# A linear-attention and MLP kernel: new load order and head-half work in the first batch, other slots for batch 3, a 384+128 last chunk

## The chip, the cores and the metric

The kernel runs on one core of a Trainium2 chip. The metric is the device time of one execution in microseconds; of several runs the median is taken. Times in a profile count from the first instruction of the profiled execution; its span ends with the last instruction, and the execution's own time is a little longer.

## The reference

For 8 batches of 8 heads, 576 tokens and a head size of 64, linear attention is computed, and its output goes through a two-layer MLP with the tanh form of gelu:

```
phi(x) = where(x > 0, x, exp(x) - 1) + 1
kv  = phi(k)^T v          # per head, 64 x 64
z   = sum over tokens of phi(k)
num = phi(q) kv ;  den = phi(q) . z + 1e-6
x   = num / den           # heads side by side: 4608 tokens x 512
out = gelu_tanh(x @ w_in) @ w_out     # w_in 512 x 2048, w_out 2048 x 512
```

Inputs and output are float32; the kernel multiplies in bfloat16.

## The kernel before, in words

**Tiling.** Each batch has 512 main tokens (4 chunks of 128) and a rest of 64. The main tokens of batch b make block j = b of the MLP; the rests of all eight batches together make a ninth block of 512 tokens, block 8. The attention of a block is: exponentials on ScalarE (ACT), phi on VectorE (DVE, `phi_into`, L176: `max(x,0) + min(exp(x),1)`), a cast of v beside a column of ones (`cast_v` L204, `cast_vr` L212 for the rest), five matmuls for each of four head pairs into `kv_ps` (`kv_mm`, L220 and L227), two copies of the diagonal 64-row blocks into the block-diagonal `kvbd` (`kv_evac`, L243; `second` names another engine for the second block), transposes of phi(q) to `qt`, four matmuls for each chunk into `n_ps` (`nab_mm`, L254), a reciprocal and a product on DVE (`nab_evac`, L264 and L266), and a transpose of x to `xt`. The rests have the same steps, two batches in one tile (`plan_rest`, with the transposed `qtr` and the output `xt_rest`).

**The MLP.** `first_half(j)` makes 16 row blocks m of h: four matmuls of 512 columns each (L302), then gelu on ACT (L685). `second_half(j)` runs 16 groups of four matmuls into `o_ps` (L728), copies the result and stores it. For the last quarter of block 8 `last_chunk` makes the output in column pieces (L697, copy L706, stores L709).

**The order of the work.** It is written out by hand: each engine runs its instructions in program order, and so do the queues of SyncE (SP), which issues most loads and the transposing DMAs, and of GpSimd (POOL), which issues later loads of the rests and casts the weights (L150, L157). `at(phase, j, slot, fn)` puts attention work of later batches behind slot `slot` of `first_half(j)` (phase 1) or `second_half(j)` (phase 2); within one slot it runs in the order in which the plan functions were called. `plan_second`, `plan_third` and `plan_attention(3, ...)` place batches 1, 2 and 3; batch 3's kv and nab work stands in `first_half(2)`.

**Buffers.** Loads of k, q, v and weight stages share six buffers (`pld`, tag `ld`). PSUM has four one-bank buffers `ps_ho` and two two-bank buffers `ps_a`; in block 0, h for m = 0 to 3 goes to `ps_ho` and m = 4 to 7 to `ps_a`.

**The start.** SP issues the loads of batch 0, the first rests, batch 1's k and the first two column blocks of w_in (L113 to L123). Meanwhile `keep_warm` (L329) runs matmuls on zeros. Then exponentials, phi, transposes of q through TensorE (`transpose_q`, L337, with a copy at L338), the v cast, kv, the evacuation, nab and the transposes of x follow. `first_mm_early` makes h for the first half of the tokens. The exponentials of batch 1's k (L401, L405) stand on ACT before the gelu table is loaded (L146), and that before the first gelu. In `plan_second`, `last_w_out` casts half of the last block of w_out on ACT (L157) behind batch 1's `kv_evac`.

Of the kernel before, what the change touches and what calls it, by code (L numbers as in the profile page):

```python
# [15 lines left out]
def kernel(  # L16
# [12 lines left out]
    nc = tc.nc  # L29
# [33 lines left out]
    def load_main(src, b, name, eng, parts=1):  # L63
        t = pld.tile([P, H, C * D], FP32, name=name, tag="ld")
        hs = H // parts
        for i in range(parts):
            eng.dma_start(  # L67
                out=t[:, i * hs : (i + 1) * hs, :],
                in_=src[b, i * hs : (i + 1) * hs, 0:MAIN, :].rearrange(
                    "h (p c) d -> p h (c d)", c=C  # L70
                ),
            )
        return t

    def load_rest_half(src, t, m, s, eng):
        eng.dma_start(  # L76
            out=t[REST * s : REST * (s + 1)],
            in_=src[2 * m + s, :, MAIN:S, :].rearrange("h p d -> p h d"),
        )
# [4 lines left out]
            load_rest_half(src, t, m, s, eng)  # L84
        return t

    def load_w_in(i, parts=1):
        t = pld.tile([P, KM, 512], FP32, name="w_st", tag="ld")
        n = 512 // parts
        for u in range(parts):  # L90
            nc.sync.dma_start(  # L91
                out=t[:, :, n * u : n * (u + 1)],
                in_=w_in_r[:, :, 512 * i + n * u : 512 * i + n * (u + 1)],
            )
        return t

    def load_w_out(i):
# [18 lines left out]
    for n in ("kr", "vr", "qr"):  # L116
        ld[n, 0] = prest.tile([P, H, D], FP32, name=n[0] + "_r")
    load_rest_half(k, ld["kr", 0], 0, 0, nc.sync)
    ld["v", 0] = load_main(v, 0, "v_x", nc.sync, parts=2)
    load_rest_half(v, ld["vr", 0], 0, 0, nc.sync)  # L120
    ld["k", 1] = load_main(k, 1, "k_x", nc.sync)
    load_rest_half(k, ld["kr", 0], 0, 1, nc.sync)
    w_st = [load_w_in(0, 2), load_w_in(1)]  # L123


    ident = const.tile([P, P], BF16, name="ident")
# [210 lines left out]
            nc.tensor.transpose(t_ps[:, c, 0, :], src(c, i), ident)  # L337
        copy(out=qt[:, :, i, :], in_=t_ps[:, :, 0, :])  # L338

    for n, e, s in (  # L340
        ("k", ke, halves[0]),
        ("k", ke, halves[1]),
        ("q", qe, halves[0]),
        ("kr", kre, None),
        ("q", qe, halves[1]),
    ):
        if s is None:
            exp_rest_half(n, e, 0)
        else:
            nc.scalar.activation(e[:, s], ld[n, 0][:, s], AF.Exp)  # L350
    keep_warm(36)
    phi_into(kp, ld["k", 0], ke, halves[0])
    phi_into(kp, ld["k", 0], ke, halves[1])
    phi_into(qp, ld["q", 0], qe, halves[0])
    phi_rest_half("kr", kre, 0)
    cast_v(0, nc.scalar.copy, halves[0])
    for i in range(2):
        transpose_q(i, nc.scalar.copy)
    keep_warm(5)
    phi_into(qp, ld["q", 0], qe, halves[1])  # L360
    cast_v(0, nc.scalar.copy, halves[1])
    cast_vr(0, (0,))
    for i in range(2, NP):
        transpose_q(i, nc.vector.tensor_copy)
    keep_warm(2)
    for i in range(NP):
        if i % 2 == 0:
            kv_ps = ps_a.tile([P, 2, 512], FP32, name="kv_ps", tag="a")
        kv_mm(0, i, kv_ps, i % 2)
        if i % 2 == 1:  # L370
            kv_evac(0, kv_ps[:, 0:1], i // 2, nc.scalar.copy)
    keep_warm(1)
    for i in range(2):
        cast_w_in_halves(i)
# [22 lines left out]
    nab0(1)  # L397
    keep_warm(2)
    tx0(0)
    ke1 = pe.tile([P, H, C * D], BF16, name="k_e")  # L400
    nc.scalar.activation(ke1[:, 0:2], ld["k", 1][:, 0:2], AF.Exp)  # L401
    nab0(2)
    keep_warm(1)
    tx0(1)
    nc.scalar.activation(ke1[:, 2:H], ld["k", 1][:, 2:H], AF.Exp)  # L405
    kre1 = pe.tile([P, H, D], BF16, name="kr_e")
    exp_rest_half("kr", kre1, 1)
    gelu_table()
# [29 lines left out]
    def at(ph, j, slot, fn):  # L438
        fill.setdefault((ph, j, slot), []).append(fn)
# [66 lines left out]
            at(ph, j, s_n[c], lambda c=c: nab(c))  # L506
            at(ph, j, s_n[c], lambda c=c: tx(c))

    def plan_rest(m, j0, j1, s1):
        box = {}  # L510

        def tq():
            box["qt"] = psm.tile([P, NP, P], BF16, name="qtr")
            nc.sync.dma_start_transpose(
                out=box["qt"],
                in_=phi["qr", m][:, 0].rearrange("p h d -> p (h d)"),
            )

        def nab():
            n_ps = ps_a.tile([P, 2, 512], FP32, name="n_ps", tag="a")  # L520
            for h in range(2):
                nab_mm(box["qt"], kvbds[(2 * m + h) % 4], n_ps, slice(REST * h, REST * (h + 1)))
            x = nab_evac(n_ps)
            nc.sync.dma_start_transpose(
                out=xt_rest[:, :, P * m : P * (m + 1)],
                in_=x.rearrange("p a t d -> p (a t d)"),
            )

        at(*j0, tq)
        at(1, j1, s1, nab)  # L530

    def plan_second():

        b = 1
        box = {}

        def exps():
            box["q"] = pe.tile([P, H, C * D], BF16, name="q_e")
            for s in halves:
                nc.scalar.activation(box["q"][:, s], ld["q", b][:, s], AF.Exp)  # L540
            gelu_table()

        def phis():
            phi["q", b] = pphi.tile([P, C, H, D], BF16, name="q_p")
            for s in halves:
                phi_into(phi["q", b], ld["q", b], box["q"], s)

        def cast_vs():
            cast_vr(0, (1,))
            cast_v(b, nc.vector.tensor_copy)  # L550

        def last_w_out():
            cast_w_out_halves(3, (nc.gpsimd.tensor_copy, nc.scalar.copy))
            load_rests(1, (("kr", k), ("vr", v)))
            for s in range(2):
                load_rest_half(q, ld["qr", 0], 0, s, nc.gpsimd)
            load_rests(1, (("qr", q),))

        def kv():
            kv_ps = ps_a.tile([P, 2, 512], FP32, name="kv_ps", tag="a")  # L560
            for i in range(NP):
                kv_mm(b, i, kv_ps)
            kv_evac(b, kv_ps, second=nc.scalar.copy)

        def tq(h):
            if h == 0:
                box["qt"] = pt.tile([P, C, NP, P], BF16, name="qt")
            t_ps = ps_a.tile([P, 4, NP, P], BF16, name="t_ps", tag="a")
            t_q(q_src(b), None, 2 * h, 2, t_ps)
            copy = nc.vector.tensor_copy if h else nc.scalar.copy  # L570
            copy(out=box["qt"][:, 2 * h : 2 * h + 2], in_=t_ps[:, 0:2])

        def nab(c):
            n_ps = ps_a.tile([P, 2, 512], FP32, name="n_ps", tag="a")
            nab_mm(box["qt"][:, c], kvbds[b], n_ps)
            box["x", c] = nab_evac(n_ps)

        def tx(c):
            copy = nc.scalar.copy if c < 2 else nc.vector.tensor_copy
            pe_tx(b, c, box["x", c], c < 2, copy)  # L580

        def early(m):
            first_mm_early(1, m)

        at(1, 0, 11, exps)
        at(2, 0, 0, phis)
        at(2, 0, 0, cast_vs)
        for fn, c, slot in (
            (tq, 0, 7), (tq, 1, 7), (lambda c: kv(), 0, 10), (lambda c: last_w_out(), 0, 10),
            (nab, 0, 11), (nab, 1, 12), (nab, 2, 13), (tx, 0, 13), (nab, 3, 14),  # L590
            (tx, 1, 14), (tx, 2, 15), (early, 0, 15), (early, 1, 15), (tx, 3, 15),
            (early, 2, 15),
        ):
            at(2, 0, slot, lambda fn=fn, c=c: fn(c))
# [94 lines left out]

    def last_chunk(g, u):  # L690

        if u % 2 == 1:
            return
        o_ps = ps_ho.tile([P, d_model], FP32, name="o_ps", tag="ho")
        t, f = C - 1, slice(128 * u, 128 * u + 256)
        for m in range(MM):
            nc.tensor.matmul(  # L697
                o_ps[:, f],
                lhsT=g[:, m, P * t : P * (t + 1)],
                rhs=w_out_sb[:, m, f],  # L700
                start=(m == 0),
                stop=(m == MM - 1),
                skip_group_check=True,
            )
        o_sb = pld.tile([P, 1, 512], FP32, name="o_last", tag="ld")
        nc.vector.tensor_copy(o_sb[:, 0, f], o_ps[:, f])  # L706
        for s, eng in ((0, nc.sync), (1, nc.scalar)):
            r0 = (2 * t + s) * S + MAIN
            eng.dma_start(  # L709
                out=out[r0 : r0 + REST, f], in_=o_sb[REST * s : REST * (s + 1), 0, f]  # L710
            )
# [39 lines left out]
    plan_prepare(  # L751
        3, (2, 1, 7), (2, 1, 15), None, (1, 2, 0), (1, 2, 1), None, (2, 1, 12)
    )
    plan_attention(3, 1, 2, (4, 5, 6, 7), (11, 12, 13, 14))
    for b in range(4, B):
        j = b - 2
        plan_prepare(
            b, (1, j, 15), (2, j, 1), (2, j, 2), (2, j, 3), (2, j, 5), (2, j, 8), (2, j, 8)
        )
        plan_attention(b, 1, b - 1, (1, 2, 3, 4), (6, 8, 10, 12))  # L760
    plan_rest(0, (1, 2, 3), 2, 15)
    at(2, 1, 7, lambda: box0.__setitem__("qr", phi_rest("qr", 1)))
    at(1, 2, 8, lambda: box0["qr"]())
    plan_rest(1, (2, 2, 8), 3, 14)
    for b in range(4, B):
        at(2, b - 3, 2 if b == 4 else 0, lambda b=b: load_batch(b))
    for m in range(2, 4):
        at(2, 2 * m - 3, 3, lambda m=m: load_rests(m, (("kr", k), ("vr", v))))
        at(1, 2 * m - 2, 9, lambda m=m: load_rests(m, (("qr", q),)))
    for m in range(2, 4):  # L770
        plan_rest(m, (2, 2 * m - 2, 9), 2 * m, 14)

    for j in range(B + 1):
        first_half(j)
# [29 lines left out]
```

## Time and profile before

| what | value |
| --- | --- |
| median of 5 runs | 300.46 us (298.78 to 302.07) |
| the profiled execution | 298.78 us, its span 297.0 us |
| granted TensorE clock | 0.999 |
| first h matmul of block 0 | 20.64 us |
| first o_ps matmul of block 0 | 35.01 us |
| first half of block 2, with batch 3's attention | 85.73 to 103.72 us |
| last matmul | 293.03 us |
| DVE, ACT, POOL busy | 132.3, 159.2, 37.9 us |

In the profile PE is TensorE's matmuls and PEld its weight loads, DVE is VectorE, POOL is GpSimd, SP is SyncE, and a q behind an engine means its sequencer, which issues DMAs. A line of the timeline has start, length, engine, source line, operation, out<-in, shape and count; in brackets is the idle time before it and what ended it. Matmul lengths include the pipeline, so the array's time is read from start to start.

### The profile page before, as it was taken

The numbers are of one execution on the slowest core, as the hardware profiler recorded it, in microseconds if no ns is written. First come the engines' busy times: TensorE is split into PE (matmuls) and PEld (weight loads), VectorE is DVE, ScalarE is ACT, GpSimd is POOL, SyncE is SP. The second block draws the span as 40 slices with busy tenths as digits, with TensorE's granted clock in tenths as the row PEclk, the third lists the DMA queues.
The fourth block names the chain that finished last, engine by engine and source line by source line (L and its number), as shares of the span: only waits on it lengthen the run. The fifth ranks groups of instructions, "written<-read, shape, count | busy, mean of one in ns | idle before, by whom it ended". The sixth has DMA issues, their size and how long they took to land.

```text
span 297.0 us, 4320 instructions
## 1 busy us (share of the span) xinstructions
PE 287.8 (97%) x1698; PEld 149.8 (50%) x1698; DVE 132.3 (45%) x244; ACT 159.2 (54%) x222; POOL 37.9 (13%) x56
## 2 busy tenths in 40 slices
PE   8889999999999899999999999999999999999995
PEld 6775455644564444554455445544544444444444
DVE  2979494228689478244714493438142000000002
ACT  4658934679964572567356825682561067017500
POOL 8028658300002400000000000000000000000000
PEclk9999999999999999999999999999999999999999
DMA  7999999991498999736933696203341110021033
GB/s 250 339 379 406 392 370 372 320 373 58 112 347 248 172 237 352 163 68 202 349 108 55 194 356 142 53 20 106 106 54 36 71 71 2 0 83 58 2 71 72
DMA packets 64260, 53.24 MB, mean 179 GB/s; under 512 B 31728, under 2 KB 57584, under 8 KB 64240
## 3 DMA queue, kind: packets, MB, share of 16 engines
q1 hardware_dynamic: 60816, 41.82, 49.0%
q10 hardware_dynamic: 2464, 8.52, 7.4%
q0 software_dynamic: 960, 2.62, 3.8%
q8 instruction: 13, 0.21, 0.3%
q14 instruction: 7, 0.06, 0.1%
HBM read 36.70 MB, written 9.44 MB: 155 GB/s over the span
## 4 chain that ended last, share of the span: by engine, by line
PE 86%; DMA 5%; SPq 4%; DVE 2%; issue 1%; POOL 1%; ACT 0%; ACTq 0%
PE o_ps L728 40%; PE h_ps L302 38%; DMA w_st<-in_moe_w_in_dram 3%; PE n_ps L254 2%; SPq L67 2%; PE kv_ps L220 2%; DMA qtr<-qr_p 2%; SPq L76 2%; PE o_ps L697 1%; DVE k_p L176 1%; SPq L91 1%; PE t_ps L277 1%; PE kv_ps L227 1%; POOL w_in_sb L150 1%; DVE kvbd L243 0%
## 5 line engine op out<-in xcount | busy, mean ns | idle before, releaser
L728 PE MATMUL o_ps<-w_out_sb,g 128*128 128x512 bf16 x560 | 124.6, 379 | 0.2 <-ACT w_out_sb L157 0.2
L302 PE MATMUL h_ps<-xt,w_in_sb 128*128 128x512 bf16 (+1 forms) x548 | 119.8, 365 | 0.3
L685 ACT ACTIVATE g<-h_ps 128x512 bf16<-128x512 f32 x144 | 83.8, 598 | 50.9 <-PE h_ps L302 48.2
L728 PEld LDWEIGHTS <-g 128*128 128x128 bf16 x560 | 54.1, 98 | 63.3 <-issue 0.5
L302 PEld LDWEIGHTS <-w_in_sb 128*128 128x128 bf16 x612 | 57.6, 98 | 54.9 <-issue 0.5
L743 ACT COPY o_sb<-o_ps 128x512 f32<-128x512 f32 x18 | 10.5, 585 | 55.5 <-PE o_ps L728 55.5
L741 DVE COPY o_sb<-o_ps 128x512 f32<-128x512 f32 x17 | 11.7, 688 | 62.4 <-PE o_ps L728 62.3
L266 DVE TENSOR_TENSOR x<-n_ps,r 128x512 bf16<-128x512 f32 x36 | 24.9, 691 | 1.2
L176 DVE SCALAR_TENSOR_TENSOR k_p<-k_x,k_e 128x512 bf16<-128x512 f32 (+1 forms) x36 | 22.9, 697 | 0.3
L176 DVE SCALAR_TENSOR_TENSOR q_p<-q_x,q_e 128x512 bf16<-128x512 f32 (+1 forms) x40 | 22.4, 622 | 0.3
L264 DVE RECIPROCAL r<-n_ps 128x8 f32<-128x8 f32 x36 | 7.4, 206 | 27.4 <-PE n_ps L254 27.4
L243 DVE CAST kvbd<-kv_ps 64x260 bf16<-64x260 f32 (+1 forms) x15 | 6.1, 409 | 28.0 <-PE kv_ps L227 28.0
L172 DVE TENSOR_SCALAR k_e<-k_e 128x2048 bf16<-128x2048 bf16 (+1 forms) x9 | 5.7, 635 | 22.3 <-ACT k_e L167 17.7
L329 PE MATMUL w_ps<-warm 128*128 128x252 bf16 x94 | 13.7, 310 | 1.1 <-DVE warm L128 1.1
L254 PEld LDWEIGHTS <-qt 128*128 128x128 bf16 x128 | 9.7, 98 | 8.7 <-issue 1.4
L302 PE MATMUL h_ps<-xt_rest,w_in_sb 128*128 128x512 bf16 x64 | 14.0, 379 | 0.0
L254 PE MATMUL n_ps<-kvbd,qt 128*128 128x130 bf16 x128 | 12.7, 221 | 1.2 <-DMA qt<-q_p 0.7
L220 PEld LDWEIGHTS <-k_p 128*128 128x128 bf16 x128 | 9.7, 96 | 6.3 <-issue 0.9
L220 PE MATMUL kv_ps<-vp,k_p 128*128 128x130 bf16 x128 | 11.8, 220 | 0.6 <-DVE vp L204 0.6
L204 DVE CAST vp<-v_x 128x2048 bf16<-128x2048 f32 x7 | 8.6, 1222 | 8.7 <-DMA v_x<-in_v_dram 8.7
L150 POOL CAST w_in_sb<-w_st 128x1024 bf16<-128x1024 f32 x8 | 10.4, 1329 | 13.9 <-DMA w_st<-in_moe_w_in_dram 13.9
L146 ACT ACT_TABLE_LOAD x8 | 10.3, 1283 | 3.3 <-DVE o_sb L741 2.8
(61 smaller groups left out, 153.9 us busy)
## 6 DMA issues: line engine op xcount, KB each, us to landing
out_dram<-o_sb ACTq DMA_DIRECT2D x16, 512.0 KB, 3.5
k_x<-in_k_dram SPq DMA_DIRECT2D x7, 1024.0 KB, 6.0
v_x<-in_v_dram SPq DMA_DIRECT2D x7, 1024.0 KB, 11.7
q_x<-in_q_dram SPq DMA_DIRECT2D x6, 1024.0 KB, 9.3
w_st<-in_moe_w_out_dram SPq DMA_DIRECT2D x4, 1024.0 KB, 11.5
w_st<-in_moe_w_in_dram SPq DMA_DIRECT2D x3, 1024.0 KB, 9.3
q_x<-in_q_dram SPq DMA_DIRECT2D x4, 512.0 KB, 9.2
k_x<-in_k_dram SPq DMA_DIRECT2D x2, 512.0 KB, 4.2
```

Source lines behind the costliest of these rows:

```text
L146: nc.scalar.preload_act_table_set("gelu_apprx_tanh_and_others")
L150: nc.gpsimd.tensor_copy(out=w_in_sb[:, :, 512 * i + 256 * u : 512 * i + 256 * (u + 1)], in_=w_st[i][:, :, 256 * u : 256 * (u + 1)],)
L176: nc.vector.scalar_tensor_tensor(xp[:, c, hs, :], xv[:, c, hs, :], 0.0, ev[:, c, hs, :], op0=ALU.max, op1=ALU.add,)
L220: nc.tensor.matmul(dst, lhsT=kp[:, c, P * i : P * (i + 1)], rhs=vps[b % 2][:, 2 * i : 2 * i + 2, c, :], start=(c == 0), stop=False,)
L254: nc.tensor.matmul(n_ps[rows, i // 2, 2 * E * (i % 2) : 2 * E * (i % 2) + 2 * E], lhsT=qt_c[:, i, rows], rhs=kvbd[:, i, :], skip_group_che ...
L266: nc.vector.tensor_tensor(x, n_v[:, :, :, 0:D], r[:, :, :, None].to_broadcast([P, 2, 4, D]), op=ALU.mult,)
L302: nc.tensor.matmul(h_ps[:, tok], lhsT=w_in_sb[:, c, P * m : P * (m + 1)], rhs=xt[:, c, tok], start=(c == 0), stop=(c == KM - 1), skip_grou ...
L329: nc.tensor.matmul(w_ps[:, 0:252], lhsT=warm[:, 0:P], rhs=warm)
L685: nc.scalar.activation(gs[j][:, i, :], ps, AF.Gelu_apprx_tanh)
L728: nc.tensor.matmul(o_pss[t], lhsT=g[:, m, P * t : P * (t + 1)], rhs=w_out_sb[:, m, :], start=(m == 0), stop=(m == MM - 1),)
L741: nc.vector.tensor_copy(dst, o_ps)
L743: nc.scalar.copy(dst, o_ps)
```

## The change

It has five parts. In the first batch the rest of v is loaded ahead of v, v stays behind k and q, w_in's first block and half of its second go ahead of batch 1's k, and the other half behind it; the exponentials and phi of k's rest move behind those of q; all copies of `qt` are ACT's; and kv runs by halves of the heads, where the second half of v is cast by DVE (heads 4 and 5) and ACT (6 and 7) after the first half's evacuation. The exponential of batch 1's k is one instruction, behind both ACT copies of `xt`. `kv_evac` of batch 1 stays wholly on DVE. Batch 3's kv and nab each move one slot on, and the rest nab of batches 0 and 1 moves from slot 15 of `first_half(2)` to slot 2 of `second_half(2)`. The last chunk is made in columns 0 to 383 and 384 to 511.

```diff
-    def load_w_in(i, parts=1):
-        t = pld.tile([P, KM, 512], FP32, name="w_st", tag="ld")
-        n = 512 // parts
-        for u in range(parts):
-            nc.sync.dma_start(
-                out=t[:, :, n * u : n * (u + 1)],
-                in_=w_in_r[:, :, 512 * i + n * u : 512 * i + n * (u + 1)],
-            )
+    def load_w_in(i, t=None, f=slice(0, 512)):
+        if t is None:
+            t = pld.tile([P, KM, 512], FP32, name="w_st", tag="ld")
+        nc.sync.dma_start(
+            out=t[:, :, f], in_=w_in_r[:, :, 512 * i + f.start : 512 * i + f.stop]
+        )
         return t
...
     load_rest_half(k, ld["kr", 0], 0, 0, nc.sync)
+    load_rest_half(v, ld["vr", 0], 0, 0, nc.sync)
     ld["v", 0] = load_main(v, 0, "v_x", nc.sync, parts=2)
-    load_rest_half(v, ld["vr", 0], 0, 0, nc.sync)
+    w_st = [load_w_in(0), load_w_in(1, None, slice(0, 256))]
     ld["k", 1] = load_main(k, 1, "k_x", nc.sync)
     load_rest_half(k, ld["kr", 0], 0, 1, nc.sync)
-    w_st = [load_w_in(0, 2), load_w_in(1)]
+    load_w_in(1, w_st[1], slice(256, 512))
...
-    for n, e, s in (
-        ("k", ke, halves[0]),
-        ("k", ke, halves[1]),
-        ("q", qe, halves[0]),
-        ("kr", kre, None),
-        ("q", qe, halves[1]),
-    ):
-        if s is None:
-            exp_rest_half(n, e, 0)
-        else:
+    for n, e in (("k", ke), ("q", qe)):
+        for s in halves:
             nc.scalar.activation(e[:, s], ld[n, 0][:, s], AF.Exp)
+    exp_rest_half("kr", kre, 0)
     keep_warm(36)
-    phi_into(kp, ld["k", 0], ke, halves[0])
-    phi_into(kp, ld["k", 0], ke, halves[1])
-    phi_into(qp, ld["q", 0], qe, halves[0])
-    phi_rest_half("kr", kre, 0)
-    cast_v(0, nc.scalar.copy, halves[0])
+    for n, xp, e in (("k", kp, ke), ("q", qp, qe)):
+        for s in halves:
+            phi_into(xp, ld[n, 0], e, s)
     for i in range(2):
         transpose_q(i, nc.scalar.copy)
     keep_warm(5)
-    phi_into(qp, ld["q", 0], qe, halves[1])
-    cast_v(0, nc.scalar.copy, halves[1])
+    phi_rest_half("kr", kre, 0)
+    cast_v(0, nc.scalar.copy, halves[0])
     cast_vr(0, (0,))
     for i in range(2, NP):
-        transpose_q(i, nc.vector.tensor_copy)
+        transpose_q(i, nc.scalar.copy)
     keep_warm(2)
-    for i in range(NP):
-        if i % 2 == 0:
-            kv_ps = ps_a.tile([P, 2, 512], FP32, name="kv_ps", tag="a")
-        kv_mm(0, i, kv_ps, i % 2)
-        if i % 2 == 1:
-            kv_evac(0, kv_ps[:, 0:1], i // 2, nc.scalar.copy)
+    for h in range(2):
+        if h == 1:
+            cast_v(0, nc.vector.tensor_copy, slice(4, 6))
+            cast_v(0, nc.scalar.copy, slice(6, 8))
+        kv_ps = ps_a.tile([P, 2, 512], FP32, name="kv_ps", tag="a")
+        for i in range(2):
+            kv_mm(0, 2 * h + i, kv_ps, i)
+        kv_evac(0, kv_ps[:, 0:1], h, nc.scalar.copy)
...
     tx0(0)
-    ke1 = pe.tile([P, H, C * D], BF16, name="k_e")
-    nc.scalar.activation(ke1[:, 0:2], ld["k", 1][:, 0:2], AF.Exp)
     nab0(2)
     keep_warm(1)
     tx0(1)
-    nc.scalar.activation(ke1[:, 2:H], ld["k", 1][:, 2:H], AF.Exp)
+    ke1 = exp_main("k", 1)
...
-    def plan_rest(m, j0, j1, s1):
+    def plan_rest(m, j0, j1):
...
-        at(1, j1, s1, nab)
+        at(*j1, nab)
...
-            kv_evac(b, kv_ps, second=nc.scalar.copy)
+            kv_evac(b, kv_ps)
...
-        if u % 2 == 1:
+        if u > 1:
             return
...
-        t, f = C - 1, slice(128 * u, 128 * u + 256)
+        t, f = C - 1, (slice(0, 384), slice(384, 512))[u]
...
-    plan_attention(3, 1, 2, (4, 5, 6, 7), (11, 12, 13, 14))
+    plan_attention(3, 1, 2, (5, 6, 7, 8), (12, 13, 14, 15))
...
-    plan_rest(0, (1, 2, 3), 2, 15)
+    plan_rest(0, (1, 2, 3), (2, 2, 2))
...
-    plan_rest(1, (2, 2, 8), 3, 14)
+    plan_rest(1, (2, 2, 8), (1, 3, 14))
```

The call for m = 2 and 3 changes in the same way as that for m = 1, in form alone.

More of the change, by code (lines that the diff above doesn't have):

```diff
@@ L770 @@
     for m in range(2, 4):
-        plan_rest(m, (2, 2 * m - 2, 9), 2 * m, 14)
+        plan_rest(m, (2, 2 * m - 2, 9), (1, 2 * m, 14))
     for j in range(B + 1):
```

## The prediction

> **What bounds the kernel now.** I read the page first, then TensorE's waits, then its timeline around each wait, then the landings of the first DMAs (each issue's start plus its time to landing).
>
> The page:
>
> ```profile
> PE 287.8 (97%) x1698; PEld 149.8 (50%) x1698; DVE 132.3 (45%) x244; ACT 159.2 (54%) x222; POOL 37.9 (13%) x56
> L728 PE MATMUL o_ps<-w_out_sb,g 128*128 128x512 bf16 x560 | 124.6, 379 | 0.2 <-ACT w_out_sb L157 0.2
> ```
>
> TensorE is the bound: 97% of the span. Its matmuls overlap, so cost is start to start: 0.216 us for 512 columns (64 of them from 134.09 to 147.90), 0.109 for 256. Moving work on other engines gains nothing unless a TensorE gap closes. The waits, columns total, times, longest:
>
> ```profile
> PE n_ps L254 <- DMA qtr<-qr_p: 0.8, 1, 0.8
> PE n_ps L254 <- DMA qt<-q_p: 0.7, 1, 0.7
> PE kv_ps L220 <- DVE vp L204: 0.6, 1, 0.6
> PE o_ps L728 <- ACT w_out_sb L157: 0.2, 1, 0.2
> ```
>
> Four single waits, of which three fall into one stage, the first product of batch 2, where batch 3's attention is woven in. TensorE's timeline there (start, length, group):
>
> ```profile
> 87.68 1.67 PE L302 MATMUL h_ps<-xt,w_in_sb 128*128 128x512 bf16 x7
> 90.00 0.40 PE L220 MATMUL kv_ps<-vp,k_p 128*128 128x130 bf16 x4 [0.65 <-DVE vp L204]
> ...
> 99.64 1.02 PE L302 MATMUL h_ps<-xt,w_in_sb 128*128 128x512 bf16 x4
> 101.31 0.41 PE L254 MATMUL n_ps<-kvbd,qt 128*128 128x130 bf16 x4 [0.66 <-DMA qt<-q_p]
> 101.56 1.02 PE L302 MATMUL h_ps<-xt,w_in_sb 128*128 128x512 bf16 x4
> 103.36 0.44 PE L254 MATMUL n_ps<-kvbd,qtr 128*64 128x130 bf16 x8 [0.77 <-DMA qtr<-qr_p]
> 103.72 1.47 PE L728 MATMUL o_ps<-w_out_sb,g 128*128 128x512 bf16 x6
> ```
>
> Start to start the gaps are larger than the brackets. Seven matmuls from 87.68 are paid at 87.68+7x0.216=89.19, so kv lost 0.81; 99.64+4x0.216=100.50, so the nab for chunk 3 lost 0.82; 101.56+0.86=102.42, so the rest nab lost 0.93. Together 2.56 us.
>
> Two smaller gaps. At 48.77 o_ps waits 0.40 (47.94+2x0.216=48.37) for ACT's cast of w_out:
>
> ```profile
> 47.28 0.37 ACT L243 CAST kvbd<-kv_ps 64x260 bf16<-64x260 f32 x1 [3.70 <-DVE kvbd L243]
> 47.68 1.04 ACT L157 CAST w_out_sb<-w_st 128x1024 bf16<-128x1024 f32 x1
> ```
>
> The cast's data landed at 44.97, but ACT stood before it on kv_evac. And in the start, the chain that ended last goes
>
> ```profile
> 14.49 8.55 DMA w_st<-in_moe_w_in_dram
> 23.10 1.50 POOL w_in_sb L150
> 24.64 10.53 PE h_ps L302 x48
> ```
>
> 24 narrow matmuls from 21.74 are paid at 24.36, so w_in's second block costs 0.28. Before 20.64 the start is batch 0's attention chain, with TensorE fed by keep_warm.
>
> **What the skill says.** The Trainium skill, DMA: Bandwidth & Descriptors, "Queues, rings and completion order": on each DMA engine a ring's descriptors are taken in order. The trace agrees: SP's first sixteen transfers land in issue order (10.18, 10.96, 12.13, 13.80, 14.55, 17.45, 18.17, 19.18 ... for q, k_r, v, v, v_r, k, k_r, w_in), about 0.75 us per 128 KB rest and 2.55 per 1 MB. SBUF — State Buffer, "SBUF: two separate sides": a DVE instruction with two SBUF inputs and a GpSimd instruction exclude each other. Agrees: k_p takes 0.69 alone and 1.52 beside POOL's casts, which go from 1.04 to 1.49; PSUM-fed DVE work beside them stays at 0.69. TensorE: Matmul & The Clock Gate, "What's actually happening": the clock falls after about 3.4 us idle. The trace shows no such gap and a granted clock of 0.999.
>
> **The change, part by part.**
>
> *Batch 3 one slot on, rest nab three slots on.* kv moves from slots 4-7 to 5-8, nab from 11-14 to 12-15. TensorE reaches kv after one more h group, at 89.19+0.86=90.05; the vp cast ends at 89.95. Gap 0.81 goes, with 0.05 to spare. DVE's order (k_p, vp, q_p, qr_p, kv_evac, second qr_p) stays, and kv_evac is asked for 0.05 later, so qt's last transpose lands where it did, 101.27. Ten slots lie between kv and the last nab as before: TensorE arrives at 100.50+0.05=100.55 and still waits 0.77, until 101.31. But now h of slot 15 is behind it, and o_ps starts at 101.55. The rest nab comes after three o_ps groups, 101.55+3x0.86=104.14, past qtr's landing at 103.31: no wait. It keeps its 0.37 and its 0.09 of entry (the unstalled rest nabs of later batches show 0.09). Equivalent end 101.55+0.46=102.01 against 103.72: **-1.71**. Behind the rest nab: its evacuation (0.21+0.69) now stands on DVE after k_p and kr_p of batch 4 and before vp and q_p, and its transpose on SP after batch 5's loads and before qt. ACT's exponentials for batch 4 come about 1.9 earlier, so q_p comes 1.0 earlier nevertheless; qt landed at 121.98 for a nab at 124.91. xt_rest is used only at the end. Cost 0; 0.9 if that cover were gone.
>
> *kv_evac of batch 1 wholly on DVE.* A second DVE half takes 0.43 (batch 2: 0.42 and 0.43 back to back), ending at 46.76+0.87=47.63 against ACT's 47.65: nothing for nab. ACT, free since 43.58, casts w_out from 44.97 to 46.05; the need is 48.37. **-0.40**.
>
> *First batch.* Queue: v_r goes ahead of v, then w_in 0 and half of w_in 1, then k, k_r, the other half. Estimated landings, adding the steps above one after another from k_r's 10.96: v_r +0.75=11.7, v +1.3=13.0 and +1.6=14.6 (two halves took 2.84 with the step before), w_in 0 +2.6=17.2, half of w_in 1 +1.25=18.4, k +2.8=21.2, k_r +0.7=21.9, last half 23.05 as before, since as much lies ahead of it. ACT: exp of q's second half starts on landing, 10.2, not behind kr at 11.52; so DVE's q_p runs through from 9.53 and ends at 13.23 (14.49 before). kr_p to 14.15, vr cast to 14.49. ACT: two qt copies to 12.9, v heads 0-3 13.05-14.08 (1.03), two qt copies to 15.04. kv of the first pairs starts its last product at 14.83; evacuation, 0.32 later, on DVE 15.15-15.44, then ACT to 15.73. Only then v 4-5 on DVE (0.42, the 64x512 cast's row) to 15.82 and v 6-7 on ACT (0.58) to 16.28; kv of the last pair 16.33-16.56, evacuation 16.88-17.45. nab restarts at 17.50, not 17.26: +0.24. So halving the cast saves less than standing behind the first evacuation costs. DVE's three x follow 0.24 later; the third transposes end at 20.72. xt's second copy, no longer behind a piece of exp k (0.63 at 19.48), is ready at 20.67, so h starts at 20.72 against 20.64: +0.08. w_in's third cast (POOL, 1.04 each from 17.2) ends near 20.4, long before the 24.4 at which it is needed, and the 0.28 gap goes: **-0.20**. Both ends: -0.5 if v lands early enough for the DVE and ACT casts and the crossings between the engines are shorter than shown; +0.5 if v's first half lands 0.5 late, since ACT's cast of it then gates kv. TensorE idles 1.0 us once, far below 3.4. k late: exp k 21.2-23.1, kr to 23.7, table load 1.28 to 25.0, gelu 1.0 later than 23.94. Cover: h for m=0..7 has eight PSUM banks; m=8 starts at 27.9 and needs gelu 0 at 25.6. Later wo, q and v land as before, since the bytes ahead are the same. Phi k ends about 1 later, DVE idles 4.3 until 34.76.
>
> *Last chunk 384+128.* Matmuls 16x(0.163+0.058)=3.53 against 3.49 (0.163 between the measured widths, 0.058 from kv's 130 columns): +0.04. Last copy 0.29 (the 64x130 row) against 0.42; half the last store: up to -0.2. Together **-0.1**. The unshown 32 KB store: between no gain and 0.3.
>
> Sum -1.71-0.40-0.20-0.10=-2.4: span 297.0 to 294.6, this execution 298.78 to 296.4. It was the fastest of the five, 1.7 under the median; from the median 300.46 I get 298.0.
>
> **Rivals.**
>
> *B: a batch 3 wait only moves.* The margin at kv is 0.05, and transposes shown take 2.4 to 7.5 us to land, beside POOL's loads. If qt's last lands 0.9 later, the total is -1.5: 299.0. For: the wait for qt stays even in my sum, and the title says two slots where the diff moves one. Against: its issue follows an unchanged DVE order.
>
> *C: qt lands sooner.* If it lands 0.8 sooner, all 2.56 go, total -3.2: 297.3. A second slot would have given this; for it speaks only the scatter of landings.
>
> *D: slower, by the first batch.* v is last of the attention inputs and its second half gates kv. Once it lands after about 15.4 plus, each us is one us for TensorE; slower than before needs 15.4+2.4=17.8. It would have to lag its place in the queue by 3 us. Price at 18.8: +1.0, 301.5.
>
> **Chances.** Mine 0.57 (own range 297.2 to 298.9), B 0.20, C 0.18, D 0.05. Medians of this kernel scatter by some 0.7, so the range is 296.3 to 300.0. One per cent, about what a measurement can tell from no change, is 3.0 us: faster means under 297.46. That is two thirds of C and a third of mine: 0.30. Slower 0.03, within 0.67.
>
> **What would show it.** Right: no wait of kv on vp and of n_ps on qtr near 90-103, one of 0.6-0.7 on qt; w_out_sb cast by ACT ending near 46; h at 24.4 with no POOL wait; nab of batch 0 at about 17.5. Wrong: h waiting for ACT's gelu near 28, kv waiting for v past 16.5, a new wait in batch 4.

## The result and the profile after

Over the runs of one comparison the changed kernel takes 297.4 us (25 runs, 295.67 to 299.97) and the kernel before 299.41 us (46 runs, 297.1 to 302.97). The ratio is 0.994, with a 95% interval of 0.992 to 0.9959: faster by 1.8 us, between 1.2 and 2.4. The forecast was 298.0 from a median of 300.46, a ratio of 0.992, which lies at the edge of that interval. The ratios here and below, and the medians of the experiments, are over the runs in the fast state alone: beside the experiments 43 of 168 runs of the kernel before were in a slower one, of the kernel after none of 36, and no run here shows why. The profiled execution took 296.17 us with a span of 294.4, against 298.78 and 297.0. The two single profiles thus differ by 2.6 us, a little more than the ratio says.

TensorE is still the bound. The page's busy row and its costliest group:

```profile
PE 286.8 (97%) x1698; PEld 149.2 (51%) x1698; DVE 132.2 (45%) x244; ACT 159.7 (54%) x222; POOL 37.0 (13%) x56
L718 PE MATMUL o_ps<-w_out_sb,g 128*128 128x512 bf16 x560 | 124.6, 379 | 0.0
```

TensorE's work is the same to the instruction: 1698 matmuls, and the 560 of the output product sum to 124.6 again (L728 has become L718). Of that group only the idle time ahead of it went, from 0.2 to 0.0. So the gain has to be in the waits. Beside the first wait of `keep_warm`, these are all of TensorE's (columns total, times, longest):

```profile
PE kv_ps L219 <- DVE vp L203: 0.8, 1, 0.8
PE t_ps L276 <- DVE x L265: 0.6, 2, 0.4
PE n_ps L253 <- ACT kvbd L242: 0.3, 1, 0.3
PE n_ps L253 <- DVE kvbd L242: 0.2, 1, 0.2
PE kv_ps L219 <- ACT vp L203: 0.2, 1, 0.2
```

The waits for qtr, qt and w_out_sb have no row any more. A row of kv on vp is still there, even larger, and it is another wait: the timeline puts it at 16.00, in batch 0, where the change has kv wait for the second half of the v cast. All of these rows lie in the first batch. Line and tile name an instruction of the program, not its place in time. In the stage of batch 3 the timeline shows

```profile
87.73 2.11 PE L301 MATMUL h_ps<-xt,w_in_sb 128*128 128x512 bf16 x9
89.67 0.40 PE L219 MATMUL kv_ps<-vp,k_p 128*128 128x130 bf16 x4
...
99.30 1.02 PE L301 MATMUL h_ps<-xt,w_in_sb 128*128 128x512 bf16 x4
100.40 0.41 PE L253 MATMUL n_ps<-kvbd,qt 128*128 128x130 bf16 x4
100.65 2.75 PE L718 MATMUL o_ps<-w_out_sb,g 128*128 128x512 bf16 x12
103.33 0.43 PE L253 MATMUL n_ps<-kvbd,qtr 128*64 128x130 bf16 x8
103.69 1.47 PE L718 MATMUL o_ps<-w_out_sb,g 128*128 128x512 bf16 x6
```

At 0.216 us each, start to start, nine h matmuls from 87.73 are paid (the array is done with them) at 87.73+9x0.216=89.67, where kv starts: no gap. From 99.30 four are paid at 100.16, and nab starts at 100.40: 0.24 is left of the wait for qt, too short for a bracket or a row of the waits. The rest nab stands behind three groups of o_ps and waits for nothing. The cast of w_out that cost 0.40 at 48.77 runs as soon as its data is there:

```profile
43.98 1.04 ACT L156 CAST w_out_sb<-w_st 128x1024 bf16<-128x1024 f32 x1 [0.38 <-DMA w_st<-in_moe_w_out_dram]
```

In the start, TensorE's rows and one of the chain are

```profile
16.00 0.39 PE L219 MATMUL kv_ps<-vp,k_p 128*128 128x130 bf16 x4 [0.78 <-DVE vp L203]
17.73 0.51 PE L253 MATMUL n_ps<-kvbd,qt 128*128 128x130 bf16 x6 [0.34 <-ACT kvbd L242]
20.95 1.04 PE L301 MATMUL h_ps<-xt,w_in_sb 128*128 128x256 bf16 x8
```

```profile
22.21 12.98 PE h_ps L301 x72
```

The chain runs through h from 22.21 to 35.19 with no landing of w_in and no POOL cast ahead of its row block 4, as it had before. But nab of batch 0 goes on at 17.73 instead of 17.26, and h starts 0.31 later.

Added up from instants of the two traces: the first full-width h of row block 4 is at 24.67 against 24.64 (+0.02). The gap for w_out is gone (-0.40). The stage of batch 3, from the first h matmul of `first_half(2)` (85.35, before 85.73) to the first o_ps of block 2, takes 15.30, and 0.46 for the rest nab that now stands behind it, against 17.99 (-2.23). From the first matmul of the last chunk to the end of the span it is 7.36 against 7.37 (-0.01). Together -2.6, the difference of the spans.

### The profile page after: what moved, and what is told of

It is laid out like the page before. It is cut to its first block, busy times and chain, and to the rows that moved or that the text cites. A ratio compares the mean times of both kernels' runs of the same rounds, so it can differ in the third digit from the quotient of the medians.

```text
span 294.4 us, 4318 instructions
## 1 busy us (share of the span) xinstructions
PE 286.8 (97%) x1698; PEld 149.2 (51%) x1698; DVE 132.2 (45%) x244; ACT 159.7 (54%) x222; POOL 37.0 (13%) x56
## 4 chain that ended last, share of the span: by engine, by line
PE 86%; DVE 7%; DMA 3%; issue 1%; ACT 1%; DVEq 0%
PE o_ps L718 41%; PE h_ps L301 38%; PE n_ps L253 3%; PE kv_ps L219 2%; DMA qt<-q_p 2%; DVE q_p L175 2%; DVE k_p L175 2%; DMA k_x<-in_k_dram 1%; PE o_ps L687 1%; DVE kvbd L242 1%; PE t_ps L276 1%; DVE x L265 1%; DVE k_e L171 1%; PE kv_ps L226 1%; DVE q_e L171 0%
## 5 line engine op out<-in xcount | busy, mean ns | idle before, releaser
L718 PE MATMUL o_ps<-w_out_sb,g 128*128 128x512 bf16 x560 | 124.6, 379 | 0.0
L718 PEld LDWEIGHTS <-g 128*128 128x128 bf16 x560 | 54.1, 98 | 62.7
L175 DVE SCALAR_TENSOR_TENSOR q_p<-q_x,q_e 128x512 bf16<-128x512 f32 (+1 forms) x40 | 23.9, 660 | 0.3
L175 DVE SCALAR_TENSOR_TENSOR k_p<-k_x,k_e 128x512 bf16<-128x512 f32 (+1 forms) x36 | 22.0, 673 | 0.3
L171 DVE TENSOR_SCALAR k_e<-k_e 128x2048 bf16<-128x2048 bf16 (+1 forms) x9 | 6.6, 734 | 27.4 <-ACT k_e L166 22.7
L166 ACT ACTIVATE k_e<-k_x 128x2048 bf16<-128x2048 f32 x7 | 13.4, 1911 | 0.1
L328 PEld LDWEIGHTS <-warm 128*128 128x128 bf16 x94 | 10.0, 110 | 2.9 <-DVE warm L127 1.1
## 6 DMA issues: line engine op xcount, KB each, us to landing
v_x<-in_v_dram SPq DMA_DIRECT2D x7, 1024.0 KB, 11.8
```

The costliest lines, as they stand in the source:

```text
L166: nc.scalar.activation(e, ld[name, b], AF.Exp)
L175: nc.vector.scalar_tensor_tensor(xp[:, c, hs, :], xv[:, c, hs, :], 0.0, ev[:, c, hs, :], op0=ALU.max, op1=ALU.add,)
L328: nc.tensor.matmul(w_ps[:, 0:252], lhsT=warm[:, 0:P], rhs=warm)
L718: nc.tensor.matmul(o_pss[t], lhsT=g[:, m, P * t : P * (t + 1)], rhs=w_out_sb[:, m, :], start=(m == 0), stop=(m == MM - 1),)
```

## The experiments

The first five kernels put single parts of the change into the kernel before, or take parts out of the kernel after. All medians stand against runs of the kernel before on the same chip (299.34 us for E1 to E4, 299.30 for E5 to E8, 299.01 for E9 to E12), and differences in us are worked out from the ratios. Diffs are shortened where a line is "...".

### E1: batch 3's part alone

```diff
...
-    plan_attention(3, 1, 2, (4, 5, 6, 7), (11, 12, 13, 14))
+    plan_attention(3, 1, 2, (5, 6, 7, 8), (12, 13, 14, 15))
...
-    plan_rest(0, (1, 2, 3), 2, 15)
+    plan_rest(0, (1, 2, 3), (2, 2, 2))
...
```

> The kernel before with batch 3's kv and nab one slot on and the rest nab three slots on, nothing else. My theory: this is most of the change; -1.7 us if qt's last transpose lands as in the trace of before, up to -2.5 if it lands earlier; ratio 0.992 to 0.995. No wait of kv on vp and none on qtr in the trace, one of 0 to 0.8 on qt. Rival (the gain comes from the start): ratio 0.998 to 1.000.

296.78 us, ratio 0.9927 (0.9904 to 0.995): -2.2 us, between -2.9 and -1.5. Of the three waits one is left:

```profile
PE n_ps L254 <- DMA qt<-q_p: 0.5, 1, 0.5
```

From start to start its gap is 0.67, the prediction had 0.77. By its ratio this part alone gives as much as the whole change.

### E2 and E3: its two halves

E2 has only the first pair of lines of E1's diff, E3 only the second.

> The kernel before with batch 3's kv and nab one slot on, the rest nab where it was, right behind the last nab. My theory: the two edits are not additive. kv's wait of 0.8 goes, but TensorE then reaches the rest nab an h group sooner, and the wait for qtr grows from 0.9 to about 1.8 us: 0.0 us, ratio 0.999 to 1.001. Rival (each edit is worth its own wait): -0.8 us, ratio 0.997.

> The kernel before with only the rest nab moved into the second product. My theory: the wait for qtr of 0.8 to 0.9 goes and the waits of kv (0.8) and of nab on qt (0.8) stay: -0.85 us, ratio 0.996 to 0.998. Rival (a moved rest nab delays batch 4 through DVE's queue): a new wait in block 3, no gain.

E2: 298.60 us, ratio 0.9969 (0.9937 to 1.0002). The waits for vp and qt are gone, and the one for qtr has grown:

```profile
102.20 0.41 PE L254 MATMUL n_ps<-kvbd,qt 128*128 128x130 bf16 x4
104.14 0.43 PE L254 MATMUL n_ps<-kvbd,qtr 128*64 128x130 bf16 x8 [1.54 <-DMA qtr<-qr_p]
```

The four nab matmuls at 102.20 are paid at 102.43, the rest nab starts at 104.14: 1.70, where it had been 0.93. TensorE reaches the rest nab sooner and waits there for the same landing. In this execution that landing came 16.81 after the stage began, in the profile of before 17.58, and for that reason alone the stage is shorter all the same (17.22 against 17.99); at 17.58 nothing would have been won. The ratio lies where the rival had it (0.997), but its interval takes in no change too, so the time alone doesn't separate the theories. E3: 298.44 us, ratio 0.997 (0.9946 to 0.9994), -0.9 us: qtr's gap of 0.93 went, the gaps for vp (0.81) and qt (0.82) stayed.

```profile
PE n_ps L254 <- DMA qt<-q_p: 0.7, 1, 0.7
PE kv_ps L220 <- DVE vp L204: 0.6, 1, 0.6
```

What one half leaves, the other removes: 0.9 each, 2.2 together, which is their sum within the intervals.

### E4: the start alone

E4 is the kernel after with the lines of E1 taken back, batch 1's `kv_evac` again split over two engines, and the last chunk again in two halves.

> The kernel before with only the first-batch part: load order, exponential order, qt copies on ACT, kv by head halves, one exponential of batch 1's k. My theory after the result: the attention chain gets 0.3 us longer (first h near 20.95) and the 0.28 us wait for w_in goes, so h of row block 4 starts within 0.1 us of 24.64: 0.0 us, ratio 0.998 to 1.002. Rival (the prediction as it stood): -0.2 us. Rival (the new load order is a gain of its own): -0.5 us or more.

299.73 us, ratio 1.002 (0.9993 to 1.0047): +0.6 us, between -0.2 and +1.4. The first batch's edits bring no gain that the time shows. In this execution the old layout of batch 3 lost more than in the profile of before:

```profile
PE n_ps L253 <- DMA qt<-q_p: 1.4, 1, 1.4
PE n_ps L253 <- DMA qtr<-qr_p: 1.2, 1, 1.2
```

qt was waited for 0.7 in the profile of before and qtr 0.8, with the same placement. These landings scatter between executions, and the old layout pays for each late one.

### E5: batch 1's evacuation alone

```diff
-            kv_evac(b, kv_ps, second=nc.scalar.copy)
+            kv_evac(b, kv_ps)
```

> The kernel before with only kv_evac of batch 1 wholly on DVE. My theory: ACT casts its half of w_out on landing near 45 to 46 instead of 47.7 to 48.7, the 0.40 us gap of o_ps at 48.8 goes, nab of batch 1 starts within 0.05 of 47.70: -0.4 us, ratio 0.998 to 0.999. Rival (the gap is hidden by later waits): 0.0 us at the start of block 1's second product.

298.66 us, ratio 0.9975 (0.9944 to 1.0007). The ratio says -0.75 us, the interval takes in zero. The trace shows the wait itself: the row of o_ps waiting for w_out_sb is gone, and nothing stands in its place. So that the 0.40 is won is read from the trace; the time alone doesn't show it.

### E6: both v casts ahead of the first evacuation

The prediction held that the second half of v gets late because its casts stand behind the first evacuation. E6 moves them ahead of it in the kernel after.

```diff
+    cast_v(0, nc.vector.tensor_copy, slice(4, 6))
+    cast_v(0, nc.scalar.copy, slice(6, 8))
     for h in range(2):
-        if h == 1:
-            cast_v(0, nc.vector.tensor_copy, slice(4, 6))
-            cast_v(0, nc.scalar.copy, slice(6, 8))
```

> The changed kernel with both casts of v's second half moved ahead of the first evacuation. My theory: the order, not the landing of v, costs the start 1 us: DVE casts heads 4 and 5 near 14.6 to 15.0, nab of batch 0 restarts near 16.7 instead of 17.7, first h near 19.9 instead of 20.95. Against the changed kernel -0.4 to -1.0 us (transposes of batch 1's q may then wait for DVE), against before ratio 0.988 to 0.993. Rival (v or w_in lands too late): first h stays over 20.6.

295.78 us, ratio 0.9897 (0.9844 to 0.9951). DVE, then TensorE:

```profile
14.61 0.41 DVE L203 CAST vp<-v_x 128x512 bf16<-128x512 f32 x1
15.36 0.29 DVE L242 CAST kvbd<-kv_ps 64x130 bf16<-64x130 f32 x1 [0.33 <-PE kv_ps L226]
15.95 0.29 DVE L242 CAST kvbd<-kv_ps 64x130 bf16<-64x130 f32 x1 [0.30 <-PE kv_ps L226]
```

```profile
16.59 0.51 PE L253 MATMUL n_ps<-kvbd,qt 128*128 128x130 bf16 x6 [0.32 <-ACT kvbd L242]
19.80 0.38 PE L301 MATMUL h_ps<-xt,w_in_sb 128*128 128x256 bf16 x2
```

The cast is at 14.61, ahead of both evacuations. In the kernel after, DVE made it at 15.54, between them, and the second evacuation came at 17.10. nab goes on at 16.59 instead of 17.73, and h starts at 19.80 instead of 20.95. The last q_p ended at 13.44 in one and at 13.40 in the other, so both start from the same instant. In the trace this order is worth 1.1 us; the interval overlaps that of the kernel after.

### E7, E8 and E9: the last wait for qt, both together, and k sooner

E7 puts batch 3's last nab, with its transpose, behind the first group of o_ps, which is the second slot that rival C speaks of. E8 is E6 and E7 together. E9 is E8 with batch 1's k and the rest of k loaded ahead of w_in's second block.

```diff
-            at(ph, j, s_n[c], lambda c=c: nab(c))
-            at(ph, j, s_n[c], lambda c=c: tx(c))
+            to = (2, j, s_n[c] - 16) if s_n[c] > 15 else (ph, j, s_n[c])
+            at(*to, lambda c=c: nab(c))
+            at(*to, lambda c=c: tx(c))
...
-    plan_attention(3, 1, 2, (5, 6, 7, 8), (12, 13, 14, 15))
+    plan_attention(3, 1, 2, (5, 6, 7, 8), (12, 13, 14, 16))
```

> The changed kernel with batch 3's last chunk of nab, and its transpose, one slot further: behind the first group of the second product. My theory: what is left of the wait for qt (0.24 in the trace after, 0.77 in my sum) goes: -0.2 to -0.8 us against the changed kernel, against before ratio 0.990 to 0.994. Rival (the wait moves to the next transpose or batch 4's DVE chain): no gain, a new wait past 101.

> The changed kernel with both edits, the casts of v's second half ahead of the first evacuation and batch 3's last nab one slot further. My theory: they lie in different stages and add up: -0.6 to -1.6 us against the changed kernel, against before ratio 0.986 to 0.992. Rival: an earlier start is given back in batch 1, whose loads are fixed by the queue, and only the nab part stays.

> The changed kernel with the v casts ahead of the first evacuation, batch 3's last nab one slot further, and batch 1's k with its rest ahead of w_in's second block, behind its first. My theory: with the earlier start the late k sets the gelu table and then TensorE (0.66 us at row block 8 in the run before); k 1.3 us sooner removes that, and w_in's second block still comes in time: no wait of h on gelu near 28, 0 to -0.6 us against the same kernel without the last edit, ratio to the first kernel 0.984 to 0.991. Rival (w_in's second block is then late): a wait of h on POOL at row block 4.

E7: 296.43 us, ratio 0.991 (0.9881 to 0.9939). Batch 3 has no wait left in E7, E8 and E9; the stage takes 15.51 in each, with the nab work behind it added. E8: 295.64 us, ratio 0.988 (0.9846 to 0.9913). It shows the wait that the prediction had named as covered, h for gelu. ACT, then TensorE:

```profile
23.40 1.91 ACT L166 ACTIVATE k_e<-k_x 128x2048 bf16<-128x2048 f32 x1 [2.41 <-DMA k_x<-in_k_dram]
27.28 3.04 ACT L675 ACTIVATE g<-h_ps 128x512 bf16<-128x512 f32 x6
```

```profile
28.88 1.47 PE L301 MATMUL h_ps<-xt,w_in_sb 128*128 128x512 bf16 x6 [0.49 <-ACT g L675]
```

k landed at 23.38 in this execution, so the first gelu came at 27.28, and h of m=8 lost 0.66 for want of a free buffer. So a first gelu by about 26.6 would have been in time; the prediction had said 25.6, with an h that began 0.33 sooner than here. E9: 296.20 us, ratio 0.9883 (0.9842 to 0.9925). k landed at 20.72 there, the first gelu came at 24.76, and h had no such wait; w_in's second block was still in time. The intervals of E8 and E9 are nearly the same, so the wait is shown in the trace, and its price is within what the runs scatter.

### E10: the kernel after once more

> The changed kernel as it is, as a control beside the improved ones: ratio 0.992 to 0.996; slower than the kernel with all three further edits by 0.5 to 2 us. Rival (the further edits are worth nothing): the same time.

297.1 us, ratio 0.9925 (0.9889 to 0.996), beside E9's 296.2 in the same comparison. The stage of batch 3 had no wait for qt, where the first profile of the same program had 0.24 and E1 0.67. Against that stood a wait from the scatter of the weights' loads:

```profile
PE o_ps L718 <- POOL w_out_sb L156: 0.4, 1, 0.4
```

### E11: the load order alone

E11 is the kernel before with the new order of the first loads, and nothing else.

> The kernel before with only the new order of loads. My theory: the parts of the start are tied. Batch 1's k lands near 21 instead of 17.5, and a piece of its exponential still stands on ACT ahead of xt's second copy, so the first h waits for it: first h near 22, +0.8 to +1.8 us, ratio 1.002 to 1.006. Rival (the load order is a gain alone): the w_in wait goes, -0.3 us or more.

301.03 us, ratio 1.0067 (1.0034 to 1.0101): slower by 2.0 us. ACT shows why:

```profile
20.69 0.58 ACT L390 COPY xt<-t_ps 128x512 bf16<-128x512 bf16 x1 [1.89 <-PE t_ps L276]
22.66 0.63 ACT L400 ACTIVATE k_e<-k_x 128x512 bf16<-128x512 f32 x1 [1.38 <-DMA k_x<-in_k_dram]
23.20 0.57 ACT L390 COPY xt<-t_ps 128x512 bf16<-128x512 bf16 x1
```

The piece of batch 1's exponentials waits until 22.64 for k, now late in the queue, and the second copy of xt stands behind it; h starts at 23.81, 1.64 after TensorE was ready. The new load order needs the new place of that exponential: without it, it costs time.

This execution shows one thing more. TensorE's granted clock was 0.84, 0.50 and 0.81 from 15 to 17, 17 to 19 and 19 to 21 us; in the two microseconds before, it had been busy for 0.79. Up to then its longest idle time, once it had begun, was 0.95 us, at 13.89. The start of h hangs on k's landing and was not set by this.

### E12: the rests' loads away from the transposes

The loads of the last pair of rests (m = 3) are written far behind batch 3's stage, but POOL runs ahead and issues them in it, from 95.90 to 99.27 us in the profile of before. E12 is the kernel before, where SP issues these loads later.

```diff
...
-    for m in range(2, 4):
-        at(2, 2 * m - 3, 3, lambda m=m: load_rests(m, (("kr", k), ("vr", v))))
-        at(1, 2 * m - 2, 9, lambda m=m: load_rests(m, (("qr", q),)))
+    at(2, 1, 3, lambda: load_rests(2, (("kr", k), ("vr", v))))
+    at(1, 2, 9, lambda: load_rests(2, (("qr", q),)))
+    at(2, 3, 3, lambda: load_rests(3, (("kr", k), ("vr", v), ("qr", q)), nc.sync))
```

> The kernel before with the loads of the last two batches' rests issued by SyncE one block later, so that six of the eight rest loads that GpSimd issues at 94 to 100 us are away from there. My theory: those loads are why the last transposes of batch 3's phi(q) and of the rest's take 5.5 to 6.2 us to land; without them they land in under 4, the waits of nab on qt and on qtr shrink from 0.8 and 0.9 to under 0.3 each: -1.0 to -1.7 us, ratio 0.994 to 0.997. Rival (the transposes are slow on their own or by the loads of batches): the waits stay.

298.4 us, ratio 0.9963 (0.994 to 0.9986): -1.1 us. DMA issues from 88 to 106 us, with the median time to landing last, of before:

```profile
q_r<-in_q_dram POOLq DMA_DIRECT2D x4, 128.0 KB, 4.6
qt<-q_p SPq DMA_TRANSPOSE x4, 3.7
xt<-x SPq DMA_TRANSPOSE x4, 6.0
qtr<-qr_p SPq DMA_TRANSPOSE x1, 6.2
```

And of E12:

```profile
q_r<-in_q_dram POOLq DMA_DIRECT2D x2, 128.0 KB, 3.5
qt<-q_p SPq DMA_TRANSPOSE x4, 3.7
xt<-x SPq DMA_TRANSPOSE x4, 2.4
qtr<-qr_p SPq DMA_TRANSPOSE x1, 2.5
```

With two of POOL's eight loads left in this stretch, the transposes of x and of qr land in 2.4 and 2.5 us instead of 6.0 and 6.2. The median of qt's four is 3.7 in both, because the first three are issued ahead of most of these loads and land in 2.9 to 4.2 us either way; but the last one, the one that nab waits for, lands in 3.5 instead of 5.5. Both waits for transposes are gone, and only the one for vp (0.81) stays. So the kernel before waited for qt and qtr because POOL's loads of the rests ran beside its transposes; the slots decide only whether TensorE notices. E12 changes both the queue and the time of those loads, so it doesn't tell by which of the two they disturb.

## Why the prediction was right, and where it was not

Of the instants it had named, nab of batch 0 came at 17.73 for 17.5, row block 4 at 24.67 for 24.4 and w_out's cast on ACT ended at 45.02 for 46; neither h at 28 nor batch 4 showed a new wait. The steps behind the sum fared differently.

**Batch 3: the mechanism right, the term too small.** It forecast -1.71: the gap for vp gone with 0.05 to spare, 0.77 left for qt, the gap for qtr gone. The vp gap is gone with no residue in the profile of after. qt left 0.24: its last transpose landed at 100.35, 15.0 after the start of the stage instead of 15.5, because the second of the four issues took 1.22 and not 1.76. The profile's term is -2.23, and E1's ratio says -2.2. The step that was short: the prediction took the two landings of one profile as fixed. They aren't. The length of the stage, rest nab included, in eleven profiles:

| placement | us |
| --- | --- |
| old: before, E4, E5, E11 | 17.99, 19.21, 18.26, 18.90 |
| new: after, E1, E6, E10 | 15.76, 16.19, 15.95, 15.51 |
| nothing waited for: E7, E8, E9 | 15.51 |

Against the last row the old placement loses 2.5 to 3.7 us, the new one 0 to 0.7; the means are 18.6 and 15.85, a gain of 2.7. The profile of before, on which the prediction rests, happened to be the mildest of its four. Rival C (qt lands sooner) is thus no other outcome: E10 shows it and E1 shows the prediction's own case, in the same layout. Rival B (a wait that only moves) is what E2 did with half the edit; the whole edit didn't.

**The evacuation of batch 1: right.** -0.40 in the sum, 0.40 in the trace, ACT's cast ending at 45.02 against an expected 46.05 because its data landed 1 us sooner. E5's ratio agrees, and its interval alone would not prove it.

**The first batch: its steps right, the instant they start from not.** It forecast -0.20 with ends of -0.5 and +0.5; the profile has +0.02, and E4 +0.6, between -0.2 and +1.4. Its steps:

| kernel | q landed | q_p ends | nab goes on | h starts | row block 4 |
| --- | --- | --- | --- | --- | --- |
| before | 10.18 | 14.49 | 17.26 | 20.64 | 24.64 |
| E3 (old start) | 9.79 | 13.97 | 16.74 | 20.12 | 24.12 |
| after | 9.68 | 13.40 | 17.73 | 20.95 | 24.67 |
| E10 (new start) | 10.51 | 13.52 | 17.83 | 21.05 | 24.77 |
| E4 (new start) | 11.79 | 14.79 | 19.12 | 22.34 | 26.05 |
| E7 (new start) | 11.77 | 14.78 | 19.09 | 22.31 | 26.03 |
| E6 (casts ahead) | 10.44 | 13.44 | 16.59 | 19.80 | 23.52 |
| E8 (casts ahead) | 11.68 | 14.68 | 17.83 | 21.05 | 24.77 |

The times hang on the landing of q's second half, which ranges from 9.5 to 11.8 us over all profiles, and that, not the order of instructions, makes most of the differences between rows. Counted from that landing, nab follows after 7.08 before and 7.33 in E4, which is the +0.24 of the prediction; q_p ends 1.3 sooner (3.0 after landing, 4.3 before), and the second half of v, cast behind the first evacuation, gives back 1.5 (nab 4.3 after q_p, 2.8 before). Row block 4 follows h after 3.72 instead of 4.00, which is the wait of 0.28 for w_in gone. From q's landing to row block 4 it takes 14.46 before and 14.26 in E4, E7 and E10: the -0.20 of the prediction. What failed was the instant that it all started from: the prediction took 10.18 for both kernels. In E4 and E7 q landed 1.6 later, and everything moved with it. In the profile of after it landed at 9.68, and DVE, which began q_p's second half only at 11.52 behind its own earlier work, could not use it. That work was late from its first instruction on. Its line of before, then of after:

```profile
5.60 0.46 DVE L172 TENSOR_SCALAR k_e<-k_e 128x1024 bf16<-128x1024 bf16 x1 [4.61 <-ACT k_e L350]
```

```profile
5.67 0.86 DVE L171 TENSOR_SCALAR k_e<-k_e 128x1024 bf16<-128x1024 bf16 x1 [4.67 <-ACT k_e L341]
```

It ran beside POOL's clearing of `kvbd` and `kr_p`, took twice as long, and k_p began 0.48 later. It did so in four of the fourteen profiles, with the new start (after, E4, E10) and with the old (E12), so this is scatter too. In the eight profiles with the new load order q's landing has a mean of 11.0, in the six with the old order 10.2. The loads ahead of it are the same in both, so whether the later loads delay it, or it is scatter, stays open. A landing 0.8 later, less the 0.20, would be the +0.6 of E4; no run here settles it.

**Gelu: covered, as said.** The first gelu came at 24.67, 0.7 later than before (1.0 forecast), with the table load of 1.28 right ahead of it, and h didn't wait. E8 shows where the cover ends.

**The last chunk: right over the profiles, hidden in this pair.** -0.1 forecast. From its first matmul to the end of the span it is 7.36 in the profile of after and 7.37 before. But the five other profiles with the new chunk have 7.21 to 7.31, and of the eight with the old one six have 7.37 to 7.39 and two 7.84 and 8.01. So about 0.1 is won as a rule, too little for the medians. It wasn't tried by itself.

**The clock: a margin that isn't one.** The prediction set TensorE's idle time of 1.0 us against the 3.4 us after which, by the page that it cites, the clock falls. In the profile of after the longest idle time was 0.78 us past 7 us and the clock held. In E11, though, the clock fell after no idle time over 0.95 us, and an idle time of 2.07 us at 105.60 in the same execution left it as it was. The measurement decides: a single idle time below 3.4 us is no assurance here. What does set the clock these runs don't show.

**Rival D (slower by the first batch)** asked for v to lag by 3 us. v wasn't late: kv's wait at 16.00 was for DVE's place in its own order. E11 shows the other way in which the start could have made the kernel slower, a load moved back whose consumer holds up its engine; the change had closed it.

The sum came out at -2.4, the spans differ by 2.6 and the ratio makes it 1.8. A batch 3 term that was too small was offset by a first batch that gained nothing; that the two errors nearly cancel is luck. The ratios of E1, E4 and E5 multiply to 0.9922, beside 0.994 and 0.9925 (E10) for the whole: within their intervals the parts add up. The version with both v casts ahead of the first evacuation and batch 3's last nab one group later (E8, 295.64; with k sooner, E9, 296.20) is the fastest seen, 0.9 to 1.8 us under the medians of the kernel after (297.4, and 297.1 in E10); the intervals overlap, so that much is likely and not shown.

## What to carry to other kernels

When a stage waits several times in a row, cost the waits together: an edit that removes one brings TensorE to the next one sooner, as in E2, where qtr's gap grew from 0.93 to 1.70. A wait for a DMA that one profile shows as 0.7 us is one draw of a landing that scatters; slack behind other work is worth more than that figure. An instruction that uses a late load goes behind everything on its engine that TensorE is waiting for, and a load is moved back only together with its consumer (E11). Casts that TensorE waits for go ahead of evacuations that it doesn't wait for yet (E6). Where the code places a DMA isn't when it is issued: a queue with nothing to wait for runs ahead, and its loads can slow transposes that the code shows nowhere near them (E12).

## What the runs showed of the hardware

A transposing DMA of 128 KB (the last of qt, qtr and those of x in this stage) landed in 2.4 to 3.5 us with two loads from POOL's queue near it and in 5.2 to 7.5 beside eight of them (E12 against before). SP's issue of one took 1.22 us as a rule, and in the same program position between 1.22 and 2.15 for the second of four. The Trainium skill, DMA: Bandwidth & Descriptors, "SWDGE vs HWDGE vs iDMA", says that software and hardware queues feed different queues inside each DMA engine, which the engine serves in turn; the slower landings beside POOL's loads agree with it, though no run here shows the engines' turns themselves. The second half of q, fourth of the loads from the start, landed at 9.5 to 11.8 us in the profiles, a scatter as large as the whole gain of this change. DVE's first instruction on k took 0.46 to 0.52 us in ten profiles and 0.86 to 0.96 in the four (after, E4, E10, E12) in which POOL's last clearing of `kvbd` beside it took 0.54 instead of 0.81. TensorE's clock was granted at half for 3.4 us in E11, from 16.34 us on, after no idle time over 0.95 us.
